# Where the code of three engines lies and in which order TensorE first enters it, in a decode block with a 512 MB cache

## The chip, the core and the metric

The kernel runs on one core of one Trainium2 chip, in one launch. The metric is the device time of one execution in microseconds; lower is better. Three executions of the kernel before took 1303.85 to 1303.99 us, with a median of 1303.93 us.

## The reference, cut to what matters

One decode step of a transformer block for B = 2 rows of D = 448, in float32: layer norm, attention with 16 heads of 256 over a cache of 8192 keys and values for each row, and then a second layer norm and a bilinear feed-forward layer of F = 1792.

```python
q = (layernorm(x) @ wq).reshape(B, 1, 16, 256).transpose(0, 2, 1, 3)
scores = einsum("bhqd,bhkd->bhqk", q, k_cache) * 256 ** -0.5
o = einsum("bhqk,bhkd->bhqd", softmax(scores), v_cache)
h = x + o.transpose(0, 2, 1, 3).reshape(B, 1, 4096) @ wo
n = layernorm(h)
out = h + ((n @ w_gate) * (n @ w_up)) @ w_down
```

There are 32 pairs of head and row. Each pair reads 8 MB of keys and 8 MB of values, and with the weights 561 MB have to come in.

## The kernel before, in words

All large loads are issued by SyncE on one queue, in the order in which they are needed: the first weights `w[0]`, the first quarter of the keys of pair 0 (`k0a`) and the rest of them (`k0`), the keys of pair 1, and then values and keys in turn (`loads`, L381 and L190). SyncE waits ahead of some of them until a buffer is free. A load lies over 128 partitions, and it is spread over the core's 16 DMA engines.

**Start.** ScalarE loads `x`. TensorE turns it with four small transposes (L241), VectorE and TensorE make its mean and its variance (L244 to L266), and TensorE makes the queries of the first four heads (`query`, L272 and L277), which ScalarE scales (L285). VectorE multiplies the first quarter of the keys by the first query (L358, into `vb`), and SyncE waits for that product, `product[0]`, before it issues the keys of pair 1.

**Loop.** PE, VectorE and ScalarE each run a loop over the heads. VectorE multiplies keys by the query and sums over 256 (L358, L363); TensorE and ScalarE make the softmax; TensorE multiplies by the values (`mix`, L336). The two engines hand work to each other by semaphores that are counted down again (`take`, L319).

**End.** The last two pairs are written out without a loop. Of the last pair's 64 key blocks, ScalarE sums the first `BY_ACT` = 44 by 44 single activations with an accumulated output (L529), VectorE the other 20 (L363). SyncE waits for both sums, `last_act[0]` and `summed_last`, because the last values and the weights of the feed-forward layer go into the buffer `kb`, in which the last keys lie. After that come the last values in three parts (`LAST`, on the semaphores `late`), `wg`, `wu` in two halves and `wd` in four parts (`DOWN` = 7, 4, 2, 1). TensorE's last work is the product with `wd` (L778); VectorE copies `y` (L785), and SyncE stores it (L796).

**Code and blocks.** An engine's program is loaded in blocks. The numbers that the code uses are 256 instruction slots for a block of TensorE and 128 for one of VectorE or ScalarE. In the kernel before, TensorE's loop begins at the head of its second block (`head_slot={PE: 0}`), all that stands ahead of it lies in its first block, and the end of the program follows behind the loop. VectorE's and ScalarE's code lies where it falls.

Of the kernel before, what the change touches and what calls it, by code (L numbers as in the profile page):

```python
# [4 lines left out]
AF = mybir.ActivationFunctionType  # L5
ALU = mybir.AluOpType
AX = mybir.AxisListType
PE, DVE, ACT = (getattr(mybir.EngineType, n) for n in ("PE", "DVE", "Activation"))

B, D, H, SK, DH, F = 2, 448, 16, 8192, 256, 1792  # L10
EPS = 1e-5
P = 128
HALF = 64
DC = 4
# [3 lines left out]
HC = 16  # L18
# [9 lines left out]
BY_ACT = 44  # L28
# [45 lines left out]
def decode_block(nc, x, k_cache, v_cache, w, wg, wu, wd, out):  # L74
# [4 lines left out]


    names = ("x", "w", "k0", "k1", "k0a", "v", "g", "p", "d", "a", "zero", "dp", "ap", "pd", "pa", "da")
    names += ("dd", "aa", "gp", "first", "mixed", "heads")
    S = {n: Sem(nc, n) for n in names}
    late = [Sem(nc, f"late{i}") for i in range(len(LAST) + 1 + 2 + len(DOWN))]
    done = Sem(nc, "out")
    pe, dve, act, sp, pool = (
        Engine(e) for e in (nc.tensor, nc.vector, nc.scalar, nc.sync, nc.gpsimd)
    )

    def p_(instr):  # L90
        return S["p"].by(instr)

    def v_(instr):
        return S["d"].by(instr)

    def a_(instr):
        return S["a"].by(instr)
# [4 lines left out]
    def place(name, shape, offset=None):  # L102
        size = 4
        for n in shape[1:]:
            size *= n
        if offset is None:
            offset = at[0]
            at[0] += -(-size // 32) * 32
        return nc.alloc_sbuf_tensor_at(name, list(shape), F32, offset=offset).ap()
# [9 lines left out]
    ident = place("ident", (P, P))  # L119
# [3 lines left out]
    s_t = [place(f"s{i}", (P, NJ)) for i in range(2)]  # L123
# [15 lines left out]
    x_sb = place("x_sb", (B, DC * P))  # L139
# [30 lines left out]
    xT_ps = banks[6][:, : DC * B].rearrange("p (c b) -> p c b", b=B)  # L170
# [9 lines left out]
    def k_at(i, lo=0, hi=NJ):  # L180
        first = i % 2 * (NJ - OVER)
        return kb[:, first + lo : first + hi, :]


    x_in = S["x"].by(nc.scalar.dma_start(x_sb[:, :D], x.rearrange("b s d -> (b s) d")), 16)
    w_in = {0: S["w"].by(nc.sync.dma_start(wb[:, WQ:], w[0][:, WQ:]), 16)}

    def load_k(i, lo=0, hi=NJ, sem=None):
# [6 lines left out]
    t = S["g"].by(nc.gpsimd.memset(ident, 0.0))  # L195
    pool.wait(t)
    g_id = S["g"].by(
        nc.gpsimd.affine_select(
            out=ident, in_=ident, compare_op=ALU.not_equal, fill=1.0, base=0,
            pattern=[[-1, P]], channel_multiplier=1,  # L200
        )
    )
# [33 lines left out]
    )  # L236
    dve.wait(x_in)
    t = v_(nc.vector.tensor_copy(x_sb[:, D:], x_sb[:, D - HALF : D]))
    pe.wait(g_id, x_in, t)
    for c in range(DC):  # L240
        got = nc.tensor.transpose(xT_ps[:, c, :], x_sb[:, c * P : (c + 1) * P], ident[:B, :B])  # L241
    t = p_(got)
    dve.wait(t)
    t = v_(nc.vector.tensor_copy(xT, xT_ps))  # L244
    dve.wait(t)
    t = over_chunks(sum_x, xT)
    pe.wait(v_ones, t)
    t = p_(nc.tensor.matmul(mean_ps, ones, sum_x, start=True, stop=True))
    dve.wait(t)
    t = v_(  # L250
        nc.vector.scalar_tensor_tensor(
            xc, mean_ps[:, None, :].to_broadcast([P, DC, B]), -1.0 / D, xT,
            op0=ALU.mult, op1=ALU.add,
        )
    )
    dve.wait(t, g_xb)
    x_spread = spread(xb, xc, P)
    t = v_(nc.vector.tensor_mul(sq, xc, xc))
    dve.wait(t)
    t = over_chunks(sum_sq, sq)  # L260
    pe.wait(t)
    t = p_(nc.tensor.matmul(var_ps, ones, sum_sq, start=True, stop=True))
    act.wait(t, v_eps)
    t = a_(nc.scalar.activation(std, var_ps, AF.Sqrt, bias=eps_t, scale=1.0 / D))
    dve.wait(t)
    t = v_(nc.vector.reciprocal(rstd, std))  # L266
# [47 lines left out]
    def behind(i, k):  # L314

        return S["p"], P0 + ORDER.index((i - (NQ - B), k)) + 1

    def take(e, sem, n=1):
        e.wait_ge(S[sem].h, n).then_inc(S[sem].h, -n)  # L319

    def tell_of(instr, sem):
        instr.then_inc(S[sem].h, 1)
# [10 lines left out]
    def mix(lo, hi, v, own=0):  # L333
        for t in range(lo // 2, hi // 2):
            g, j = 32 * (t % 4), 2 * t - lo
            got = nc.tensor.matmul(  # L336
                o_ps[own][g : g + 2, :], p_t[own][:, 2 * t : 2 * t + 2], v[:, j : j + 2, :],
                start=(t < 4), stop=(t >= NJ // 2 - 4),
            )
        return got  # L340
# [12 lines left out]
    last_act = []  # L353
    last = NQ - 1
    queries = qb.rearrange("p h b d -> p (h b d)")

    def keys_times(kt, q, to=None):
        return nc.vector.tensor_mul(  # L358
            kt if to is None else to, kt, q[:, None, :].to_broadcast([P, kt.shape[1], DH])
        )  # L360
# [55 lines left out]
    first = v_(summed(0, NJ - HC, NJ, vb[:, :HC, :]))  # L416
    take(nc.vector, "k0", 16)
    t = v_(keys_times(k_at(0, 0, NJ - HC), qb[:, 0, 0]))
    dve.wait(t)
    t = v_(summed(0, 0, NJ - HC, k_at(0, 0, NJ - HC)))  # L420
# [4 lines left out]
    with nc.Fori(0, H - 1, engines=[DVE]) as g:  # L425
        for n in (1, 2):
            b = n % B
            off = nc.vector.snap((g + n // 2) % HEADS * (B * DH))
            q = queries[:, bass.ds(off + b * DH, DH)]
            parts = ((0, HC), (HC, NJ)) if b else ((NJ - HC, NJ), (0, NJ - HC))  # L430
            kt = k_at(n, *parts[0])
# [8 lines left out]
            kt = k_at(n, *parts[1])  # L440
# [7 lines left out]
    t = v_(  # L448
        nc.vector.tensor_reduce(
            sel16, ident.rearrange("p (g b r) -> p b r g", b=B, r=R)[:, :, 0, :],  # L450
            axis=AX.X, op=ALU.add,
        )
    )
# [5 lines left out]
    t = v_(  # L459
        nc.vector.tensor_scalar(  # L460
            share, sel16[:, None, :].to_broadcast([P, DC + 1, B]), -1.0 / D, None, op0=ALU.mult
        )
    )
# [12 lines left out]
    q = qb[:, (H - 1) % HEADS, B - 1]  # L476
    take(nc.vector, "k1", 16)
    dve.wait(behind(last - 1, 0))
    told["nm", last - 1] = v_(negated())
    ready = [v_(keys_times(k_at(last, 0, HC), q))]  # L480
    dve.wait(behind(last - 1, 2))
    d_rl[last - 1] = v_(nc.vector.reciprocal(rl_t[0], l_ps))
    for lo in range(HC, NJ, HC):
        ready.append(v_(keys_times(k_at(last, lo, lo + HC), q)))
    dve.wait(ready[-1])
    summed_last = v_(summed(last, BY_ACT, NJ, k_at(last, BY_ACT, NJ)))


# [1 line left out]
    with nc.Fori(0, H - 1, engines=[ACT]) as g:  # L490
        for b in range(B):
# [9 lines left out]
            got = turned_out(b, 0)  # L501
        tell_of(got, "ap")
        off = nc.scalar.snap(g % HEADS * (B * DH))
        for b in range(B):
            take(nc.scalar, "pa")
            got = nc.scalar.activation(  # L506
                queries[:, bass.ds(off + b * DH, DH)], q_ps[b], AF.Copy, scale=rstd[:, b : b + 1]
            )
# [14 lines left out]
        told["oT", i] = a_(turned_out(k, k))  # L523

    ends(last - 1)
    for k in range(BY_ACT):
        act.wait(ready[k // HC])
        kt = k_at(last)[:, k, :]
        t = a_(nc.scalar.activation(kt, kt, AF.Copy, accum_out=s_t[1][:, k : k + 1]))  # L529
    last_act.append(t)  # L530
    summed_at[last] = summed_last
    dve.wait(last_act[0], summed_last)
    told["m", last] = v_(highest(last))
# [6 lines left out]
        nc.gpsimd.sem_inc(S["gp"].h, HEADS)  # L540


    with nc.Fori(0, H - 1, engines=[PE], head_slot={PE: 0}) as g:
        with nc.Fori(0, B, engines=[PE]):
            take(nc.tensor, "dp")
            tell_of(top(), "pd")
            take(nc.tensor, "dp")
            tell_of(bias(), "pa")
            take(nc.tensor, "ap")
            tell_of(whole(), "pd")  # L550
            take(nc.tensor, "v", 16)
            tell_of(mix(0, NJ, vb), "pa")
            take(nc.tensor, "ap")
            tell_of(turned(), "pa")
        take(nc.tensor, "ap")
        take(nc.tensor, "gp")
        off = nc.tensor.snap(g % HEADS * WH)
        for c in range(2):
            nc.tensor.matmul(  # L559
                acc_ps, oT.rearrange("p c b r -> p c (b r)")[:, c], wb[:, bass.ds(off + c * D, D)],  # L560
                start=False, stop=False,
            )
        for b in range(B):
            tell_of(query(off, b), "pa")
# [4 lines left out]
    v_parts, lo = [], 0  # L569
    for n in LAST:  # L570
# [3 lines left out]
        to = kb[:, lo : lo + n, :]  # L574
# [9 lines left out]
    wd_in, lo = {}, 0  # L584
# [44 lines left out]
    pe.wait(told["p", last])  # L629
    p_(whole())  # L630
    p_(mix(56, NJ, vb[:, 56:]))
    pe.wait(v_o)
    for k, (lo, hi, v, there) in enumerate(v_parts[:-1]):
        pe.wait(there)
# [11 lines left out]
    lo, hi, v, there = v_parts[-1]  # L646
# [24 lines left out]
    def group(w, q):  # L671
# [8 lines left out]
        start=True, stop=False,  # L680
    )
    dve.wait(t_hq)
    t = v_(nc.vector.tensor_mul(mean_h, share, total[:, None, :].to_broadcast([P, DC + 1, B])))  # L683
    pe.wait(t)
    t = p_(
        nc.tensor.matmul(
            xc_ps.rearrange("p c b -> p (c b)"), ones, mean_h.rearrange("p c b -> p (c b)"),
            start=False, stop=True,
        )
    )  # L690
# [9 lines left out]
    t = v_(nc.vector.tensor_copy(xc_h, xc_ps[:, :DC]))  # L700
    dve.wait(t)
    t = v_(nc.vector.tensor_mul(sq_h, xc_h, xc_h))
    dve.wait(t)
    t = over_chunks(sum_h, sq_h)
# [30 lines left out]
        )  # L735

    t_var = []
    pe.wait(t_xr, wg_in, v_blank)
    t_g = project(g_ps, wg_t, FG, variance)
    dve.wait(t_var[0])  # L740
    t = v_(nc.vector.tensor_scalar_add(ve, varh_ps, EPS))
# [30 lines left out]
    for k in range(NF):  # L772
        n, g = FF[k]
# [3 lines left out]
        for q in range(YN):  # L777
            got = nc.tensor.matmul(  # L778
                y_ps[32 * q : 32 * q + 32, :],
                hmT[n // 2][:, n % 2, g].rearrange("p b r -> p (b r)"),  # L780
                wd_t[:, k, q * YW : (q + 1) * YW], start=False, stop=(k == NF - 1),
            )
    t = p_(got)
    dve.wait(t)
    t = v_(nc.vector.tensor_copy(y, y_ps))  # L785
# [10 lines left out]
    t = done.by(nc.sync.dma_start(rows, eight(y)), 16)  # L796
# [60 lines left out]
```

## Time and profile before

| | |
|---|---|
| median of three runs | 1303.93 us (1303.85 to 1303.99) |
| the profiled execution | 1303.78 us |
| its span, from the first to the last instruction | 1302.5 us |
| VectorE busy | 1121.5 us, 86% of the span |
| TensorE busy (matmuls) | 494.4 us, 38% |
| ScalarE busy | 86.9 us, 7% |
| moved by DMA | 561.31 MB, 431 GB/s over the span |

The profiled execution took 1.28 us more than its span. Its time is 0.15 us below the median of the runs. Names such as `bank` stand for PSUM tiles, `kb` and `vb` for the buffers of keys and values, `wb` for attention weights. The suffix q (SPq, ACTq, PEldq) means the part of an engine that issues its instructions.

### The profile page before, as it was taken

The page shows a single profiled execution, that of the slowest core. Times are in us where ns is not written, and L with a number is a line of the kernel's source. Part 1 is how long each engine was busy: PE and PEld are TensorE (multiplying, and loading weights), DVE is VectorE, ACT ScalarE, POOL GpSimd, SP SyncE. Part 2 cuts the span into 40 slices and gives each one's busy share as a digit, 9 for nine tenths or more (in the row PEclk, how much of TensorE's full clock was granted, in tenths as well). Part 3 has the DMA queues.
Part 4 walks back from the last instruction along what each step waited for, and adds up shares of the span by engine and source line. Part 5 has one row for each costly group of instructions (what it writes and reads, how often), then busy time and mean ns, then how long its engine had stood idle before and what let it go on. Part 6 is the DMA issues. An engine that isn't in the chain of part 4 may idle for free. (4 is left out here: it accounts for less than half of the span.)

```text
span 1302.5 us, 7994 instructions
## 1 busy us (share of the span) xinstructions
PE 494.4 (38%) x3182; PEld 200.4 (15%) x3182; DVE 1121.5 (86%) x272; ACT 86.9 (7%) x293; POOL 1.3 (0%) x8
## 2 busy tenths in 40 slices
PE   5034314343331433415343043432334333253548
PEld 5011102111110111202121021210112001020213
DVE  5998888889988699888899868998888897888970
ACT  2000000000000000000000000000000000000060
POOL 0000000000000000000000000000000000000000
PEclk9566657676666765667676576765667666676668
DMA  9999999999999999999999999999999999999998
GB/s 409 447 425 433 427 443 421 449 421 449 421 449 435 419 441 429 429 441 421 449 421 449 435 421 449 419 443 427 433 437 423 431 451 427 431 439 423 447 416 368
DMA packets 11412, 561.31 MB, mean 431 GB/s; under 512 B 1290, under 2 KB 1420, under 8 KB 1676
## 3 DMA queue, kind: packets, MB, share of 16 engines
q1 hardware_dynamic: 11400, 561.20, 99.7%
q8 instruction: 5, 0.08, 0.0%
q14 instruction: 3, 0.02, 0.0%
q10 hardware_dynamic: 4, 0.00, 0.0%
HBM read 561.19 MB, written 0.01 MB: 431 GB/s over the span
## 5 line engine op out<-in xcount | busy, mean ns | idle before, releaser
L358 DVE TENSOR_TENSOR kb<-kb,qb 128x12288 f32<-128x12288 f32 (+1 forms) x65 | 551.4, 8486 | 125.8 <-DVEq L319 125.7
L363 DVE TENSOR_REDUCE s<-kb 128x48 f32<-128x12288 f32 (+2 forms) x62 | 539.6, 8704 | 4.4
L336 PE MATMUL bank<-vb,p 128*2 128x512 f32 x1984 | 284.2, 734 | 408.5 <-PEq L319 408.5
L336 PEld LDWEIGHTS bank<-vb,p 128*2 128x2 f32 x1984 | 53.2, 96 | 610.6 <-issue 610.5
L328 PE MATMUL bank<-nm,ones 1*128 1x1 f32 x64 | 17.1, 334 | 202.8 <-PEq L319 202.4
L498 ACT ACTIVATE o_sb<-bank 128x512 f32<-128x512 f32 x30 | 17.9, 597 | 693.8 <-ACTq L319 693.8
L272 PE MATMUL bank<-wb,xb 128*128 (+1 forms) x228 | 60.7, 405 | 0.8 <-DMA wb<-in_w_dram 0.8
L325 PE MATMUL bank<-ident,m 128*1 128x128 f32 x32 | 10.3, 322 | 111.3 <-PEq L319 111.3
L328 PEld LDWEIGHTS bank<-nm,ones 1*128 1x128 f32 x64 | 15.3, 294 | 212.2 <-issue 210.8
L272 PEld LDWEIGHTS bank<-wb,xb 128*128 128x128 f32 x228 | 42.6, 201 | 19.9 <-issue 14.4
L345 PE MATMUL bank<-sel,o_sb 128*128 128x1 f32 x256 | 32.8, 249 | 29.9 <-PEq L319 29.1
L345 PEld LDWEIGHTS bank<-sel,o_sb 128*128 128x128 f32 x256 | 31.0, 191 | 58.8 <-issue 57.1
L559 PE MATMUL bank<-wb,oT 128*32 x60 | 32.6, 677 | 14.4 <-PEq L319 14.4
L331 PE MATMUL bank<-lsum,ones 128*128 128x1 f32 x64 | 17.4, 342 | 30.6 <-PEq L319 29.9
L372 ACT ACTIVATE nb<-bank 128x1 f32<-128x1 f32 x32 | 5.5, 171 | 330.0 <-ACTq L319 325.1
L277 PEld LDWEIGHTS bank<-wb,xb 128*128 128x128 f32 x152 | 23.7, 197 | 2.2
L277 PE MATMUL bank<-wb,xb 128*128 (+1 forms) x152 | 23.7, 279 | 0.0
L331 PEld LDWEIGHTS bank<-lsum,ones 128*128 128x128 f32 x64 | 15.6, 302 | 33.3 <-issue 32.4
L506 ACT ACTIVATE qb<-bank,rstd 128x256 f32 x30 | 14.2, 474 | 92.6 <-ACTq L319 92.6
L325 PEld LDWEIGHTS bank<-ident,m 128*1 128x1 f32 x32 | 2.6, 82 | 114.5 <-issue 114.5
L529 ACT ACTIVATE kb<-kb 128x256 f32<-128x256 f32 x44 | 17.6, 405 | 3.4 <-DVE kb L358 3.4
L683 DVE TENSOR_TENSOR mean_h<-share,total 128x10 f32<-128x10 f32 x1 | 0.2, 170 | 14.8 <-ACT hq L675 14.8
(100 smaller groups left out, 135.1 us busy)
## 6 DMA issues: line engine op xcount, KB each, us to landing
wb<-in_w_dram SPq DMA_DIRECT2D x3, 3584.0 KB, 37.5
kb<-in_A_k_cache_dram SPq DMA_DIRECT2D x1, 6144.0 KB, 25.3
kb<-in_A_v_cache_dram SPq DMA_DIRECT2D x1, 4096.0 KB, 31.9
wb<-in_w_dram SPq DMA_DIRECT2D x2, 1792.0 KB, 20.1
kb<-in_B_w_gate_dram SPq DMA_DIRECT2D x1, 3136.0 KB, 20.8
kb<-in_A_v_cache_dram SPq DMA_DIRECT2D x1, 3072.0 KB, 11.8
kb<-in_A_k_cache_dram SPq DMA_DIRECT2D x1, 2048.0 KB, 11.2
vb<-in_B_w_up_dram SPq DMA_DIRECT2D x1, 1792.0 KB, 20.0
```

Source lines behind the costliest of these rows:

```text
L272: nc.tensor.matmul(q_ps[b], xb[:, c, b, :], wb[:, bass.ds(off + WQ + c * DH, DH)], start=(c == 0), stop=False,)
L277: got = nc.tensor.matmul(q_ps[b][:, k * P : (k + 1) * P], xb[:, DC - 1 + k, b, :], wb[:, bass.ds(off + WQ + (DC - 1) * DH, P)], start=Fals ...
L328: return nc.tensor.matmul(nb_ps, ones[:1, :], nm, start=True, stop=True)
L331: return nc.tensor.matmul(l_ps, ones, lsum, start=True, stop=True)
L336: got = nc.tensor.matmul(o_ps[own][g : g + 2, :], p_t[own][:, 2 * t : 2 * t + 2], v[:, j : j + 2, :], start=(t < 4), stop=(t >= NJ // 2 - 4),)
L345: got = nc.tensor.matmul(oT_ps[:, c : c + 1], o_sb[:, (2 * k + c) * P : (2 * k + c + 1) * P], sel[:, k : k + 1], start=(k == 0), stop=(k = ...
L358: return nc.vector.tensor_mul(kt if to is None else to, kt, q[:, None, :].to_broadcast([P, kt.shape[1], DH]))
L363: return nc.vector.tensor_reduce(s_t[i % 2][:, lo:hi], kt, axis=AX.X, op=ALU.add)
L498: tell_of(nc.scalar.activation(o_sb, o_ps[0], AF.Copy), "ap")
L506: got = nc.scalar.activation(queries[:, bass.ds(off + b * DH, DH)], q_ps[b], AF.Copy, scale=rstd[:, b : b + 1])
L529: t = a_(nc.scalar.activation(kt, kt, AF.Copy, accum_out=s_t[1][:, k : k + 1]))
L559: nc.tensor.matmul(acc_ps, oT.rearrange("p c b r -> p c (b r)")[:, c], wb[:, bass.ds(off + c * D, D)], start=False, stop=False,)
```

## The change

Four things are changed. VectorE's and ScalarE's code begins 128 slots behind a boundary of 256, that is in a second block of 128, by `addr_align` with an `offset` of 128; ScalarE's load of `x` stands ahead of that. TensorE begins with a branch into its third block, goes on from there to its fourth (`look`), and then to the head of its second block, where the four transposes of `x` now stand; from there it goes back to where it began, and runs the rest in order. `head_slot` of its loop goes from 0 to 20, behind that code. Where the program comes past the two landing places, it branches over them. VectorE now waits for the transposes on a semaphore `xt`. ScalarE's 44 activations become a loop of 11 turns with 4 activations each, which takes one count of `ka` a turn; VectorE raises `ka` by 4, 4 and 3 with its products. VectorE's and SyncE's waits for ScalarE's sums are on a semaphore `summed` with 11 counts.

```diff
     x_in = S["x"].by(nc.scalar.dma_start(x_sb[:, :D], x.rearrange("b s d -> (b s) d")), 16)
+    nc.vector.addr_align(256, offset=128, max_nops=0)
+    nc.scalar.addr_align(256, offset=128, max_nops=0)
+
+    def goto(label, here=None):
+        nc.br(label, engines=[PE])
+        if here is not None:
+            nc.switch_bb(here, parent=None)
+
+    def look(k, to):
+        goto(f"behind{k}", f"block{k}")
+        nc.tensor.wait_ge(S["g"].h, 1)
+        goto(to, f"behind{k}")
+
+    goto("block2", "start")
     w_in = {0: S["w"].by(nc.sync.dma_start(wb[:, WQ:], w[0][:, WQ:]), 16)}
...
-    pe.wait(g_id, x_in, t)
-    for c in range(DC):
-        got = nc.tensor.transpose(xT_ps[:, c, :], x_sb[:, c * P : (c + 1) * P], ident[:B, :B])
-    t = p_(got)
-    dve.wait(t)
+    x_there = (g_id, x_in, t)
+    dve.wait((S["xt"], 1))
...
-    ready = [v_(keys_times(k_at(last, 0, HC), q))]
+    keys_times(k_at(last, 0, HC), q).then_inc(S["ka"].h, HC // 4)
...
     for lo in range(HC, NJ, HC):
-        ready.append(v_(keys_times(k_at(last, lo, lo + HC), q)))
-    dve.wait(ready[-1])
+        got = keys_times(k_at(last, lo, lo + HC), q)
+        if lo < BY_ACT:
+            got.then_inc(S["ka"].h, min(HC, BY_ACT - lo) // 4)
+    dve.wait(v_(got))
...
-    for k in range(BY_ACT):
-        act.wait(ready[k // HC])
-        kt = k_at(last)[:, k, :]
-        t = a_(nc.scalar.activation(kt, kt, AF.Copy, accum_out=s_t[1][:, k : k + 1]))
-    last_act.append(t)
+    flat_k = k_at(last).rearrange("p j d -> p (j d)")
+    with nc.Fori(0, BY_ACT // 4, engines=[ACT]) as g:
+        take(nc.scalar, "ka")
+        to = nc.scalar.snap(g * 4)
+        off = nc.scalar.snap(g * (4 * DH))
+        for k in range(4):
+            kt = flat_k[:, bass.ds(off + k * DH, DH)]
+            got = nc.scalar.activation(kt, kt, AF.Copy, accum_out=s_t[1][:, bass.ds(to + k, 1)])
+        tell_of(got, "summed")
+    last_act.append((S["summed"], BY_ACT // 4))
...
-    with nc.Fori(0, H - 1, engines=[PE], head_slot={PE: 0}) as g:
+    nc.tensor.addr_align(256, max_nops=0)
+    goto("queries", "block1")
+    for sem, n in x_there:
+        nc.tensor.wait_ge(sem.h, n)
+    for c in range(DC):
+        got = nc.tensor.transpose(xT_ps[:, c, :], x_sb[:, c * P : (c + 1) * P], ident[:B, :B])
+    tell_of(got, "xt")
+    turn = nc.alloc_registers("turn", engines=[PE])
+    nc.regs_mov(turn, 0)
+    nc.br_lt(turn, 1, on_true="start", on_false="queries", engines=[PE])
+    nc.switch_bb("queries", parent=None)
+    with nc.Fori(0, H - 1, engines=[PE], head_slot={PE: 20}) as g:
...
     p_(mix(56, NJ, vb[:, 56:]))
+    look(2, "block3")
     pe.wait(v_o)
...
     t_var = []
+    look(3, "block1")
     pe.wait(t_xr, wg_in, v_blank)
```

The rows below are the instructions of an engine in the order in which they stand in its program, with the line that makes them, what they write and read, and how often they repeat. First, TensorE ahead of its loop in the kernel before: the transposes of `x` are its first work, and behind the last matmul (`x_acc`, L302) come an alignment and the entry of the loop.

```order
L241 MATMUL bank<-ident,x_sb 128x2 x4
L248 MATMUL bank<-sum_x,ones 128x2
L262 MATMUL bank<-sum_sq,ones 128x2
L272 MATMUL bank<-wb,xb 128x256 x3
...
L302 MATMUL bank<-x_sb,rows 32x448
L543 ISA
L543 UNCONDITIONAL_BRANCH
L544 UNCONDITIONAL_BRANCH
```

The same place in the changed kernel.

```order
L194 UNCONDITIONAL_BRANCH
L264 MATMUL bank<-sum_x,ones 128x2
...
L318 MATMUL bank<-x_sb,rows 32x448
L566 ISA
L194 UNCONDITIONAL_BRANCH
L571 MATMUL bank<-ident,x_sb 128x2 x4
L575 COMPARE_AND_BRANCH
L577 ISA
L577 UNCONDITIONAL_BRANCH
L578 UNCONDITIONAL_BRANCH
```

The transposes now stand behind `x_acc`, at the head of the second block, and are reached by branches. Next, TensorE behind the loop in the changed kernel, at the two places where it branches over a landing place (each L194 row holds that branch and the landing place's own).

```order
L352 MATMUL bank<-vb,p_59 2x512 x4
L194 UNCONDITIONAL_BRANCH x2
L352 MATMUL bank<-kb,p_60 2x512 x16
...
L721 MATMUL bank<-mean_h,ones 128x10
L694 MATMUL bank<-wb,oT 32x112 x4
L194 UNCONDITIONAL_BRANCH x2
L754 MATMUL bank<-kb,xb 32x512 x2
```

The matmuls around them are those of before, in the same order. Last, ScalarE between the softmax of the pair before the last and that of the last pair, before:

```order
L372 ACTIVATE nb<-bank 128x1
L375 ACTIVATE p_59,lsum<-s_57,nb 128x64
L529 ACTIVATE kb,s_58<-kb 128x256 x44
L372 ACTIVATE nb<-bank 128x1
L375 ACTIVATE p_60,lsum<-s_58,nb 128x64
```

And now, where an ISA row sets an address from a register:

```order
L545 UNCONDITIONAL_BRANCH
L551 ISA
L551 REGISTER_ALU
L551 ACTIVATE kb,s_58<-kb 128x256
L551 ISA
L551 ACTIVATE kb,s_58<-kb 128x256
...
L545 REGISTER_ALU
L545 COMPARE_AND_BRANCH
```

The 44 activations have become a body of 4 (two of the four are left out here), with four such address rows, a register sum, the loop's own sum and its branch.

## Rows read from the trace of the kernel before

**Rows 1.** Page: span, share of the 16 DMA engines in 40 slices, bytes.
```profile
span 1302.5 us, 7994 instructions
DMA  9999999999999999999999999999999999999998
HBM read 561.19 MB, written 0.01 MB: 431 GB/s over the span
```

**Rows 2.** Chain that ended last: start us, us, what; its last pieces.
```profile
1271.19 28.21 DMA vb<-in_wd_dram
...
1299.44 0.99 PE bank L778 x24
...
1300.46 0.28 DVE y L785
```

**Rows 3.** Page, DMA queues: packets, MB, share of 16 engines.
```profile
q8 instruction: 5, 0.08, 0.0%
q14 instruction: 3, 0.02, 0.0%
```

**Rows 4.** Queues in 28.8-28.9, 1261.6-1261.7, 1294.0-1294.1, 1299.7-1299.9, 1273.4-1273.6 us (packets begun there).
```profile
q8 instruction: 1, 0.02, 64.2%
q8 instruction: 1, 0.02, 63.5%
q8 instruction: 1, 0.02, 67.1%
q8 instruction: 1, 0.02, 31.6%
q14 instruction: 1, 0.01, 10.0%
```

**Rows 5.** DMA view of 1296 to 1302 us, GB/s in 40 slices of 0.15 us.
```profile
GB/s 311 454 311 430 502 358 526 311 442 311 359 382 353 257 215 173 167 120 119 111 99 72 48 0 0 109 0 0 0 0 0 0 0 0 0 0 0 0 0 3
```

**Rows 6.** Line L543, TensorE's loop, its branch: ns min/median/max, first and last start.
```profile
L543 PEldq COMPARE_BRANCH  x16: 83/218/315, 25.1 to 1235.6; - x16
```

**Rows 7.** Windows, 1257.9 us to the end: busy us (x instructions) of each engine.
```profile
1257.90:1302.50 44.60, 39.00 (x415) 15.63 (x415) 11.09 (x26) 7.75 (x32) 0.00 (x0) 0.84 0.91 384
```

**Rows 8.** Timeline of the first 30 us: start, us, instruction [idle before <-releaser].
```profile
0.74 0.39 SPq L186 DMA_DIRECT2D wb<-in_w_dram  x1
1.19 16.02 SPq L190 DMA_DIRECT2D kb<-in_A_k_cache_dram  x3
2.45 0.55 PE L241 MATMUL bank<-ident,x_sb 2*128 2x2 f32 x4 [2.45 <-DVE x_sb L238]
7.58 2.93 PE L272 MATMUL bank<-wb,xb 128*128 128x256 f32 x6 [0.79 <-DMA wb<-in_w_dram]
12.43 4.43 DVE L358 TENSOR_TENSOR vb<-kb,qb 128x4096 f32<-128x4096 f32 x1 [5.15 <-DMA kb<-in_A_k_cache_dram]
27.08 12.96 DVE L358 TENSOR_TENSOR kb<-kb,qb 128x12288 f32<-128x12288 f32 x1 [5.22 <-DVEq L319]
```

**Rows 9.** DMA view of 0 to 2 us, 40 slices of 0.05 us.
```profile
DMA  0000000000000000000000000000000002099999
```

**Rows 10.** Lines L529, L490, L506 on ScalarE: ns min/median/max, first and last start.
```profile
L529 ACT ACTIVATE kb<-kb x44: 400/404/417, 1244.6 to 1261.8; 128x256 f32<-128x256 f32 x44
L490 ACTq COMPARE_BRANCH  x15: 40/45/50, 132.1 to 1239.0; - x15
L506 ACTq FUSED_REGOPS  x30: 52/69/96, 130.2 to 1238.8; - x30
```

**Rows 11.** Timeline of 1222 to 1265 us: VectorE's last sums, SyncE's loads around them.
```profile
1235.66 28.30 SPq L381 DMA_DIRECT2D kb<-in_A_v_cache_dram  x3
...
1257.64 5.49 DVE L363 TENSOR_REDUCE s<-kb 128x20 f32<-128x5120 f32 x1
...
1264.01 0.43 SPq L581 DMA_DIRECT2D kb<-in_B_w_gate_dram  x1
```

**Rows 12.** Page, DMA issues: KB, us from issue to landing.
```profile
kb<-in_A_v_cache_dram SPq DMA_DIRECT2D x1, 4096.0 KB, 31.9
```

More of the change, by code (lines that the diff above doesn't have):

```diff
@@ L81, in decode_block @@
     names = ("x", "w", "k0", "k1", "k0a", "v", "g", "p", "d", "a", "zero", "dp", "ap", "pd", "pa", "da")
-    names += ("dd", "aa", "gp", "first", "mixed", "heads")
+    names += ("dd", "aa", "gp", "first", "mixed", "heads", "ka", "summed", "xt")
     S = {n: Sem(nc, n) for n in names}
```

## Prediction

> **What bounds the kernel now.** I read the page first, then the chain of waits, then the DMA queues. The page's strip has every slice but the last at 9 tenths or more of 16 DMA engines, at 431 GB/s over 1302.5 us [rows 1]. The chain that ended last goes back through the landing of `wd`, waited for over 28.21 us up to 1299.40; behind it stand only 0.99 us of TensorE and 0.28 us of VectorE and the store [rows 2]. So the time is set by when the stream of loads begins, by gaps in it, and by when its last engine is done. One of 16 engines moves 431 / 16 = 26.9 GB/s.
>
> The change touches code loading, and that is in the trace: a queue of kind "instruction" with five packets of 0.08 MB together (16 KB each), and another with three of 8 KB [rows 3]. The narrow windows place them: 16 KB at 28.8, 1261.6, 1294.0 and 1299.7 us (the fifth, at 1278.8, reads the same), 8 KB at 1273.4 (two more at 1241 and 1243). A share of 64.2% of 16 engines for 0.1 us is 1.03 us of one engine; 10.0% for 0.2 us is 0.32 us [rows 4]. In those times that engine brings no data.
>
> The end of the stream shows it. From 1298.25 us the rate is 173 GB/s, 6.4 engines; at 1298.55 to 1299.0 it is 120 to 111, some four; then 99, 72, 48, and nothing from 1299.45 [rows 5]. Four engines are late by about 1 us, and four 16 KB packets came before that; about three more are late by less, and three were of 8 KB. That is an inference from the counts. Bytes after 1297.95 us: the ten slices sum to 1381 GB/s, times 0.15 us is 207 KB, which 16 engines move in 0.48 us. Level engines would be done at 1298.43, 1.0 us earlier, and without the eight packets' own time (5.1 us of one engine before the end, a sixteenth of it is 0.3) at 1298.1. **So everything that code loading costs in this stream is 1.0 to 1.3 us, 0.1% of the time.**
>
> The Trainium skill, "Runtime: NRT & Kernel Launch", section "Instruction fetch mechanics", calls the cost of crossing a block boundary mostly hidden. By that sentence the sum would be 0. The rows agree for the engine that executes, and differ for the DMA engines by the 1 us above.
>
> **The change part by part.**
>
> *TensorE's early visits.* Its loop is entered at 25.1 us [rows 6] and a packet follows at 28.8, so I read a packet as the load of the next block when a block is entered. From 1257.9 to the end there are 415 matmul and 415 weight-load records [rows 7], 830 slots, a bit over three blocks of 256: that fits the entries behind 1261.6, 1278.8, 1294.0 and 1299.7. The change enters the third and the fourth block early, so it should move the packets of 28.8, 1261.6 and 1278.8 (blocks three to five) to the start. Nothing enters the fifth block early. The packet for the sixth, near 1294, stays, and one engine stays 1.03 us or more late to the end. The last, at 1299.7, falls behind the stream and costs nothing in either kernel.
>
> Moving a packet gains only if it leaves the stream. Data flows from 1.7 us on [rows 9]; TensorE is released at about 0.7. The issue of `w` at 0.74 had its first data 1.0 us later, so the first early packet may begin just ahead of the stream, and the others fall into it. An engine delayed at 3 us is as late at the end as one delayed at 28.8, for no slice between shows the queue empty [rows 1]. Gain: between 0 and 0.3 us (the latest engine at 1299.45 against the first of the four at about 1299.15), since one late engine suffices; I take 0.1 to 0.2.
>
> *What the visits cost at the start.* The price of a branch to a block that is not there is in no row. Bounds: from 0 to the loaded case, 28.8 - 25.1 + 1.03 = 4.8 us for each. The first has an empty queue, nearer to 1.0 + 1.0 = 2 us; the fourth block may be on its way by then. I take 4 us in all for TensorE. It then turns `x` at 6.5 instead of 2.45 us; 0.79 us of this vanish in its wait for `w` [rows 8], and the queries are some 3.2 us late. Behind them: `product[0]` at 12.43, SyncE's keys of pair 1 (the third issue ends at 1.19 + 16.02 = 17.21, so it begins at 16.9), then the values. VectorE waits for the rest of the first keys until 27.08 [rows 8], so the queue holds data until about 26.3; less 1.0 us from issue to data, the issue could come at 25.3. The cover is about 8.4 us. A delay of 3.2 costs nothing. Without that cover it would cost its full length.
>
> *VectorE and ScalarE in their second block of 128.* A branch at the start, and 8 KB packets that move from 1241 to 1273 us to the start. At 0.32 us they don't make the latest engine. 0, at most 0.3 either way.
>
> *ScalarE's loop.* Before, 44 activations ran from 1244.6 to 1261.8 us, 0.40 us apart, so four take 1.6 us. A turn adds four address settings of 69 ns and a branch of 45 [rows 10], with the count and two sums about 0.45 us of issuing. If that runs while the datapath works, 0; if none of it does, 11 x 0.45 = 5 us. The issue work is under a third of the 1.6 us, so I take 0 to 1 us. Cover: VectorE's sum ends at 1257.64 + 5.49 = 1263.13, some 0.9 us behind ScalarE, and SyncE waits for both. Of SyncE's three issues of values the last ends at 1263.96 [rows 11]; the two behind the wait begin near 1263.2. The part ahead of them landed at 1235.66 + 31.9 = 1267.6 [rows 11, 12]; its leading engines run dry about 1.8 us earlier (they lead by 1.4, and the landing is told a little late), so data must be issued by 1264.8, 1.6 us of cover. The late engines have 1.4 us more, and they set the end. ScalarE may lose 0.9 + 1.6 + 1.4 = 3.9 us before the end moves.
>
> *The two branches over the landing places* cost 83 to 315 ns on TensorE [rows 6]; from 1271 us on the chain waits for DMA [rows 2]. 0.
>
> Sum, for the profiled execution's 1303.78 us (span 1302.5 and 1.28 around it): -0.15 +- 0.3, 1303.6. The runs' median lies 0.15 above that execution: **1303.7 us**.
>
> **The rivals.**
>
> *A, the stream becomes level.* The early packets fall ahead of 1.7 us or into a part where engines have time to spare, and the one near 1294 goes too, because blocks once asked for ahead are kept in another way than I think. All 1.0 to 1.3 us come back: 1302.7 us. For it: the window before 1.7 us is empty [rows 9]. Against it: it is only 1 us long, as long as one packet, and the sixth block.
>
> *B, slower: TensorE keeps only two blocks.* Then the way back to the second block and from there to the first are misses under load. TensorE loses 2 + 1 + 4.8 + 4.8 = 12.6 us, `product[0]` about 11.5, and the keys of pair 1 come 11.5 - 8.4 = 3 us after the queue is empty: 1306.9 us. It decides from 8.4 us of delay on; below that it is invisible. The late packets would all be there again. No row shows how many blocks TensorE keeps: in the trace it never goes back further than its loop's head. The same section of the Trainium skill says that a taken branch to a target outside the current two-page window forces a fetch before execution goes on; by that sentence B is what happens. The section also gives TensorE 128 KiB, room for eight blocks, by which B doesn't. No run here shows either yet.
>
> *C, slower: ScalarE's issue work isn't hidden.* 5 us less 3.9 is 1.1 us: 1304.9. The rows' longest values (96 and 50 ns) make 5.8 us and 1305.7. It passes 0.2% only from 6.5 us on.
>
> *The change doesn't do what it says:* the late packets come in spite of the early visits. The time is then that of before, inside the forecast's own range.
>
> **How the numbers follow.** The forecast (no change, 1303.2 to 1304.2) gets 0.62, A 0.18, B 0.09, C 0.08, and 0.03 for what I haven't seen. The predicted time is the forecast's. The range goes from A's end, 1302.5, to between C's two prices, 1305.3: it holds the forecast, A and most of C, and leaves out B's upper part. 0.2% is 2.6 us, about what a measurement of this kernel can tell from no change. No case reaches 2.6 us of gain, so faster gets 0.03 of doubt alone; slower gets 0.06 of B, 0.03 of C and 0.02 of the unseen, 0.11; same the rest, 0.86.
>
> **What would show it.** Right: 16 KB packets in the first 10 us, none between 28 and 1290, one near 1294; the transposes at 4 to 8 us; `product[0]` later but no slice under 9 tenths near 26 us; the rate after 1298.5 us still that of one to four engines until 1299.2 or later; ScalarE's 44 activations done by 1263. Wrong: the keys of pair 1 issued after 25.3 us and a slice under 9 tenths behind it (B), the second part of the last values issued after 1266 us (C), or the stream ending at full rate at 1298.3 (A).

## The result and the profile after

The changed kernel takes **1306.39 us** (median of 21 runs, 1304.76 to 1308.41), the kernel before 1304.01 us in the same runs (1303.76 to 1305.09). The ratio is 1.0019, 95% interval 1.0013 to 1.0024: 2.4 us slower, above the range of the prediction. The runs also spread over 3.7 us.

The page of the profiled execution (1307.19 us) answers to [rows 1]; the chain that ended last answers to [rows 2] (start us, us, what).

```profile
span 1305.9 us, 8107 instructions
DMA  9999999999999999999999999999999999999998
HBM read 561.19 MB, written 0.01 MB: 430 GB/s over the span
```

```profile
1273.19 29.60 DMA vb<-in_wd_dram
...
1302.83 1.00 PE bank L814 x24
...
1303.86 0.28 DVE y L821
```

The page's strip shows nothing. The stream still sets the end, and `wd` lands at 1302.79 us instead of 1299.40. So I looked for the first place where this stream is late. TensorE's branches come first, by the time in which each began (0 to 2, 4 to 5, 9 to 10.3 us, then the branch back to the start): ns min/median/max, first and last start.

```profile
L194 PEldq COMPARE_BRANCH  x1: 3842/3842/3842, 0.8 to 0.8; - x1
L194 PEldq COMPARE_BRANCH  x1: 5552/5552/5552, 4.7 to 4.7; - x1
L194 PEldq COMPARE_BRANCH  x1: 181/181/181, 10.3 to 10.3; - x1
L575 PEldq COMPARE_BRANCH  x1: 244/244/244, 10.9 to 10.9; - x1
```

The third block holds TensorE for 3.84 us and the fourth for 5.55; the two ways back cost 0.18 and 0.24. The queues of code in narrow windows answer to [rows 4]: packets begun at 1.8, 7.9, 13.7, 1294.7 and 1303.3 us (16 KB), and at 3.4 and 5.6 us (8 KB).

```profile
q8 instruction: 1, 0.02, 97.1%
q8 instruction: 1, 0.02, 55.2%
q8 instruction: 1, 0.02, 56.1%
q8 instruction: 1, 0.02, 67.1%
q8 instruction: 1, 0.02, 58.0%
q14 instruction: 1, 0.01, 12.2%
q14 instruction: 1, 0.01, 9.7%
```

Code thus moved as planned, and the packet near 1294 stayed. The timeline of the start answers to [rows 8] (start, us, instruction [idle before <-releaser]):

```profile
10.67 0.56 PE L571 MATMUL bank<-ident,x_sb 2*128 2x2 f32 x4 [10.67 <-issue]
14.93 2.91 PE L288 MATMUL bank<-wb,xb 128*128 128x256 f32 x6
19.23 4.42 DVE L374 TENSOR_TENSOR vb<-kb,qb 128x4096 f32<-128x4096 f32 x1 [3.66 <-ACT qb L301]
28.58 12.94 DVE L374 TENSOR_TENSOR kb<-kb,qb 128x12288 f32<-128x12288 f32 x1
64.01 0.33 SPq L209 DMA_DIRECT2D kb<-in_A_k_cache_dram  x1
135.72 4.42 DVE L374 TENSOR_TENSOR kb<-kb,qb 128x4096 f32<-128x4096 f32 x1 [9.88 <-DVEq L335]
```

The same two last rows in the kernel before:

```profile
62.53 0.33 SPq L190 DMA_DIRECT2D kb<-in_A_k_cache_dram  x1
133.86 4.42 DVE L358 TENSOR_TENSOR kb<-kb,qb 128x4096 f32<-128x4096 f32 x1 [9.49 <-DVEq L319]
```

VectorE's multiplication of the first keys came at 28.58 us for 27.08 [rows 8], with none of the 5.22 us of idle time ahead of it. It does not stop there: VectorE goes from one piece to the next without a pause until its first sum of pair 1, which frees the buffer, and on which SyncE waits to issue the **keys of pair 2**: 64.01 us for 62.53. The keys of pair 3, on whose landing VectorE waits, start it at 135.72 for 133.86. So 1.9 of the 3.4 us that separate the two profiled executions exist by 134 us.

Between the two lies an empty queue. A packet's row does not name its engine, but on one engine a packet begins when the one ahead of it ends, so begins and ends can be paired. By them, four engines that have brought their values of pair 0 by 66.6 us stand idle until 67.0 to 67.3, and eleven wait up to 0.4 us near 26 us, where the keys of pair 1 were issued at 23.7. Before, no engine waited over 0.01 us at either place.

The packets behind the gap are slow as well. The packets begun from 66 to 70 us (count, MB, share of 16 engines), first in the changed kernel, where 5 of the 25 are under 512 B, then in the kernel before, where 1 of the 29 is:

```profile
q1 hardware_dynamic: 25, 1.31, 90.6%
q1 hardware_dynamic: 29, 1.84, 105.9%
```

The other 20 are of 64 KB and took 2.90 us each; the 28 of before took 2.42.

The other 1.5 us of the 3.4 arise at the end. The rate from 1297 to 1303 us in 40 slices of 0.15 us answers to [rows 5]:

```profile
GB/s 382 466 335 382 442 358 382 442 406 311 478 358 430 370 388 353 221 245 155 167 119 143 143 60 131 72 119 36 36 24 24 48 24 24 24 12 24 36 24 0
```

From 1301.3 us on one engine is at work alone. Its packets, followed back, lead to the 16 KB of code at 1294.7 us, and that engine was late already: near 1259 us four engines end their 64 KB packets over 1.1 us behind the other twelve, and near 1293 us four are late again, this one among them.

### The profile page after: what moved, and what is told of

It reads as the page before. It is cut to its first block, busy times and chain, and to the rows that moved or that the text cites. A ratio compares the mean times of both kernels' runs of the same rounds, so it can differ in the third digit from the quotient of the medians.

```text
span 1305.9 us, 8107 instructions
## 1 busy us (share of the span) xinstructions
PE 499.0 (38%) x3182; PEld 201.4 (15%) x3182; DVE 1121.1 (86%) x272; ACT 86.9 (7%) x293; POOL 1.3 (0%) x8
## 5 line engine op out<-in xcount | busy, mean ns | idle before, releaser
L341 PE MATMUL bank<-ident,m 128*1 128x128 f32 x32 | 10.3, 322 | 108.1 <-PEq L335 108.1
L361 PE MATMUL bank<-sel,o_sb 128*128 128x1 f32 x256 | 32.8, 249 | 29.9 <-PEq L335 29.1
L593 PE MATMUL bank<-wb,oT 128*32 x60 | 35.6, 732 | 14.4 <-PEq L335 14.4
L347 PE MATMUL bank<-lsum,ones 128*128 128x1 f32 x64 | 17.4, 342 | 30.6 <-PEq L335 29.9
L551 ACT ACTIVATE kb<-kb x44 | 17.6, 401 | 3.6 <-ACTq L335 3.6
L385 DVE TENSOR_REDUCE nm<-bank 1x1 f32<-1x128 f32 x32 | 8.7, 272 | 4.9 <-PE bank L341 4.9
```

Source lines behind the costliest of these rows:

```text
L347: return nc.tensor.matmul(l_ps, ones, lsum, start=True, stop=True)
L361: got = nc.tensor.matmul(oT_ps[:, c : c + 1], o_sb[:, (2 * k + c) * P : (2 * k + c + 1) * P], sel[:, k : k + 1], start=(k == 0), stop=(k = ...
L551: got = nc.scalar.activation(kt, kt, AF.Copy, accum_out=s_t[1][:, bass.ds(to + k, 1)])
L593: nc.tensor.matmul(acc_ps, oT.rearrange("p c b r -> p c (b r)")[:, c], wb[:, bass.ds(off + c * D, D)], start=False, stop=False,)
```

## The experiments

Theory 1: the late issue of the keys of pair 2 (and a little of pair 1) empties the queue. Theory 2: the early packets alone make engines late, to the end. Theory 3: VectorE's and ScalarE's new code costs by itself. All runs, and from the profiled execution (us): VectorE's start on the first keys, the issue of pair 2's keys, the idle time of the 16 engines together between the last packets of pair 0's values and the next load (about 65 us; before under 0.1, after 5.4), and VectorE's start on pair 3:

| | median (range) | ratio (95%) | first keys | issue | idle | pair 3 |
|---|---|---|---|---|---|---|
| visits alone | 1305.96 (1305.24-1306.94) | 1.0015 (1.0006-1.0024) | 28.61 | 64.06 | 9.5 | 135.41 |
| rest alone | 1305.41 (1304.09-1306.94) | 1.0009 (1.0000-1.0018) | 27.62 | 63.06 | 3.9 | 134.34 |
| one visit | 1305.49 (1304.74-1306.24) | 1.0012 (1.0003-1.0021) | 28.38 | 63.82 | 8.8 | 134.75 |
| late by keys | 1307.85 (1306.85-1308.71) | 1.0028 (1.0018-1.0038) | 30.34 | 65.77 | 16.4 | 138.06 |
| late by weights | 1304.15 (1303.86-1304.75) | 1.0001 (0.9992-1.0010) | 26.99 | 62.44 | under 0.1 | 133.95 |
| idle visits | 1303.91 (1303.77-1304.54) | 1.0000 (0.9991-1.0009) | 27.25 | 62.70 | under 0.1 | 133.90 |
| three idle visits | 1303.96 (1303.68-1304.07) | 0.9998 (0.9989-1.0008) | 27.09 | 62.53 | under 0.1 | 133.91 |
| before, w first | 1303.89 (1303.74-1304.09) | 0.9999 (0.9990-1.0008) | 27.47 | 62.92 | none | 133.82 |
| after, w first | 1304.47 (1304.23-1306.25) | 1.0004 (0.9995-1.0013) | 29.29 | 64.71 | none | 134.25 |
| rest, w first | 1303.94 (1303.81-1304.21) | 0.9999 (0.9990-1.0008) | 27.54 | 62.99 | none | 133.96 |
| after, both | 1303.92 (1303.81-1304.20) | 0.9998 (0.9988-1.0007) | 28.67 | 64.11 | none | 133.71 |

The kernel before had medians of 1303.91 to 1303.95 us beside them. The interval of rest alone reaches down to no change; its loss is read together with its run with w first, below.

**Visits alone.** The kernel before with `goto("block2", "start")`, the moved transposes and the two `look` calls of the change.

> The kernel before with TensorE's early visits alone (branches into the third and fourth block, transposes of x in the second); VectorE's and ScalarE's code and ScalarE's 44 activations stay as before. Theory 1 (the two visits to absent blocks hold TensorE for 3.84 and 5.55 us, all that hangs on the queries comes late, and the load queue runs empty near 26 and 65 us): all of the loss is here, 1306.0 to 1306.8 us. Theory 2 (code packets that fall on an engine already late make the end later, whatever the start does): also 1306 or more. Theory 3 (ScalarE's loop or the place of VectorE's and ScalarE's code): 1304.0.

1305.96: 2.0 of the 2.4 us, at the low edge of what was expected. No engine waited near 26 us here, where the keys of pair 1 were issued at 23.2, so the gap near 65 us is enough.

**Rest alone.** The change without those lines.

> The changed kernel without TensorE's visits: its transposes and its loop head as before, but VectorE's and ScalarE's code in the second block of 128 and ScalarE's loop of 11 turns. Theories 1 and 2: 1303.7 to 1304.2 us, and ScalarE's activations still 0.40 us apart. Theory 3: 1306 us.

Missed: 1305.41. VectorE's rows show why, with the issue behind them:

```profile
2.74 0.18 DVE L256 COPY x_sb<-x_sb 2x64 f32<-2x64 f32 x1 [0.69 <-DMA x_sb<-in_A_x_dram]
27.62 12.96 DVE L376 TENSOR_TENSOR kb<-kb,qb 128x12288 f32<-128x12288 f32 x1 [5.21 <-DVEq L337]
63.06 0.33 SPq L208 DMA_DIRECT2D kb<-in_A_k_cache_dram  x1
```

The 5.21 us of idle time ahead of the first keys are whole, so VectorE did not come late: the keys did, by 0.54 us. Their load has landed when its latest engine is done, and by its packets that is the engine on which 8 KB of code fell at 3.54 us (the 8 KB of 5.59 us lie on another). They took 0.31 us, and the packet of data behind them 1.07 us where others of its size took 0.54, so that engine lost 0.84 us. An engine can also be late without any code: in "before, w first" the first keys came 0.39 us later than in the kernel before. With the issue at 63.06 two engines have no data until 66.3 and 67.1 us, and the spread between engines behind pair 2's keys is 2.17 us (1.79 before). The rest of this execution's loss came at the end: the 16 KB packet of TensorE's fourth block, at 1262.8 us, met an engine already 2.1 us late, and TensorE began on the second part of the last values at 1277.04 us instead of 1274.96.

```profile
1277.04 6.51 PE L354 MATMUL bank<-kb,p 128*2 128x512 f32 x32 [2.09 <-DMA kb<-in_A_v_cache_dram]
```

So theory 2 has a part, behind theory 1's.

**One visit.** The changed kernel, with the fourth block's visit taken out:

```diff
-    look(2, "block3")
+    look(2, "block1")
...
-    look(3, "block1")
```

> The changed kernel with one visit instead of two: TensorE enters the third block and goes from there to the second. Theory 1: one hold of about 3.8 us, transposes at about 5 us, product[0] no more than 3 us late, which is less than VectorE's 5.2 us of waiting before the rest of the first keys; no empty queue, 1303.7 to 1304.5 us. Theory 2: two packets (third and fourth block) still lie in the first 10 us and two more near 1279 and 1294, so 1305 to 1306.5 us.

1305.49, a time that theory 2 had named, and the first keys are waited for until 28.38, 1.3 us longer than before:

```profile
13.73 4.43 DVE L374 TENSOR_TENSOR vb<-kb,qb 128x4096 f32<-128x4096 f32 x1 [3.98 <-DMA kb<-in_A_k_cache_dram]
28.38 12.96 DVE L374 TENSOR_TENSOR kb<-kb,qb 128x12288 f32<-128x12288 f32 x1 [5.21 <-DVEq L335]
```

TensorE's lateness was within the cover here, and the early packets delayed the landing: the engine that brings the last of these keys carried 8 KB of code at 3.40 us and 16 KB at 7.52. Both theories had sent the loss down the wrong way: an early packet does not cost by being carried to the end, but by delaying the load that is waited for just then.

**Late by keys, late by weights.** No code moves. The transposes of the kernel before wait for a landing as well.

```diff
-    pe.wait(g_id, x_in, t)
+    pe.wait(g_id, x_in, t, k0a)        # late by keys
+    pe.wait(g_id, x_in, t, w_in[0])    # late by weights
```

> The kernel before, in which TensorE's transposes of x wait in addition for the landing of the first quarter of the keys (about 12.4 us instead of 2.45); no code moves, no packet of code moves. Theory 1: product[0] about 8.8 us late, so the keys of pair 1 come about 2 us after the queue is empty, and the keys of pair 2 another 1.6 us late: 1306.5 to 1307.6 us. Theory 2: 1304.0 us, since no code packet has moved.

> The kernel before, but the transposes wait for the first weights (7.4 us) too: the early chain is later by some 3.5 us and no code moves. Theory 1: VectorE idles 5.2 us ahead of the first keys, so 3.5 us are covered: the keys of pair 2 are issued at 62.5 us, 1303.8 to 1304.3. If the chain's lateness cost in proportion (5.2 us late cost 3.9 us in the run where the transposes waited for the first part of the keys): about 1306.

Late by keys made the kernel 3.9 us slower with its code where it was: the issue alone does it. Not all of it arose at 26 and 65 us: the queue runs empty once more near 1269 us (20 us of the engines together; visits alone 6.2, the changed kernel 1.1, before 0.1), behind SyncE's wait for the sums of the last keys. Late by weights, with the product for `product[0]` begun at 16.17 for 12.43, cost nothing that can be measured; 1.39 of the 5.22 us were left:

```profile
26.99 12.96 DVE L358 TENSOR_TENSOR kb<-kb,qb 128x12288 f32<-128x12288 f32 x1 [1.39 <-DVEq L319]
62.44 0.33 SPq L190 DMA_DIRECT2D kb<-in_A_k_cache_dram  x1
```

**Idle visits, three idle visits.** The transposes stay. The visits stand between TensorE's queries and its loop:

```diff
+    pe.wait(t_k0)                  # idle visits: VectorE has multiplied the first keys
+    goto("block2", "queries")      # third and fourth block; the other kernel: no wait, fifth too
```

> The kernel before with TensorE's visits to its third and fourth blocks, made only when VectorE has multiplied the first keys (about 40 us), where TensorE has nothing to do until 53 us; the transposes stay where they were. Same code packets as the visits-only kernel, two of them 35 us later. Theory 1: the start is undisturbed, the keys of pair 2 are issued at 62.5 us, no gap near 65 us, 1303.8 to 1304.4. Theory 2 (packets on engines make them late wherever they fall): 1305.3 to 1306.5.

> The kernel before with three visits of TensorE (third, fourth and fifth block) between its queries and its loop, 25 to 45 us, where it has nothing to do, so that fewer code packets fall among the last transfers. If the packet near 1294 us sets the end: 1303.0 to 1303.6. If it falls on an engine with time to spare: 1303.8 to 1304.2. If the packets at 30 to 45 us make engines late to the end: above 1304.8.

Neither costs anything. Idle visits has its packets at 45.7, 52.9 and 60.1 us, and its branches held TensorE for up to 7.87 us. Packets behind the first keys are free in these two; that refutes theory 2 in its plain form. Three idle visits has 16 KB packets at 28.8, 36.0, 43.1, 50.5 and 1299.6 us and none between the last two, and ends at the time of before: moving the packet near 1294 within the stream gains nothing.

**w first, and both.** SyncE issues the second weight load (8.8 us of stream) ahead of the keys of pair 2.

```diff
             load_v(0)
+            load_w(1)
...
-            if off == 0 and k < H // HEADS:
-                sp.wait((S["heads"], k * HEADS) if k else q_first)
+            if off == 0 and 0 < k < H // HEADS:
+                sp.wait((S["heads"], k * HEADS))
```

> The kernel before with the same exchange of two loads. In the kernel before the queue does not run empty near 65 us, though it comes close; both theories: 1303.5 to 1304.3. Above 1305 would say that the exchange itself costs, and would take its meaning from the other run.

> The changed kernel as it is, but SP issues the second weight load (3.67 MB, 8.8 us of the stream) ahead of the keys of pair 2 instead of behind them. Theory 1 (the loss is a queue that runs empty near 65 us, because the keys of pair 2 wait for VectorE's first sum of pair 1, which comes 1.5 us late): the 8.8 us in the queue cover the lateness, no gap near 65 us, 1303.8 to 1304.6. Theory 2 (the early code packets alone make engines late to the end): 1305.5 to 1307, as the changed kernel.

> The kernel with the change's rest and no visits of TensorE (it lost 1.1 us, which I had not expected), with the exchanged weight load. Theory 1: its loss too is the late issue of pair 2's keys (63.06 us for 62.53), behind first keys that landed late on the engine that the two 8 KB packets at 3.8 and 5.8 us held up: 1303.7 to 1304.2. Theory 3 (VectorE's and ScalarE's new code costs by itself): 1304.9 to 1305.6, as without the exchange.

The exchange costs the kernel before nothing, takes the rest's loss away whole, and leaves 0.6 us of the change's. The profiled execution of the latter (1306.25 us) was the slowest of its 11, so its rows show more than its median lost; engines wait up to 0.7 us near 26 us, and nowhere from 62 to 78. For that one, the last kernel also issues a quarter of the first values ahead of the keys of pair 1 (`VA` = 48):

```diff
         if n == 0:
+            load_v(0, VA, NJ, vb[:, VA:], next(sems))
             sp.wait(product[0])
...
-            load_v(0)
+            load_v(0, 0, VA, vb[:, :VA])
+            load_w(1)
```

> The changed kernel with the exchanged weight load, and with the last quarter of the first values (2.1 MB, 4.9 us of the stream, into rows that nothing uses yet) issued ahead of the keys of pair 1, so that the queue has work at 26 us as well when those keys are issued late. Theory 1 (every loss is a queue that runs empty): neither gap is left, 1303.7 to 1304.2. If the 0.5 us that the exchange alone left over come from early packets rather than from the gap near 26 us: 1304.4 again.

1303.92, as before. SyncE's issues in it, and VectorE's start on pair 3:

```profile
3.61 0.55 SPq L398 DMA_DIRECT2D vb<-in_A_v_cache_dram  x1
23.78 0.33 SPq L210 DMA_DIRECT2D kb<-in_A_k_cache_dram  x1
64.11 0.33 SPq L210 DMA_DIRECT2D kb<-in_A_k_cache_dram  x1
133.71 4.42 DVE L375 TENSOR_TENSOR kb<-kb,qb 128x4096 f32<-128x4096 f32 x1 [3.31 <-DVEq L336]
```

Both keys are issued as late as in the changed kernel, and all of its code moves are in it; the stream is no longer late. Without the two empty stretches nothing of the loss is left. (The kernel before with both exchanges was not run; w first alone gains it nothing.) No version beat the kernel before by more than can be measured.

## Why the prediction was wrong

**The step that failed is "What the visits cost at the start"**, in the first three points below, and beside it the 0 for VectorE's and ScalarE's code.

- *The price.* I took 4 us for two visits; TensorE lost 9.5 us, and `x` was turned at 10.67 us instead of my 6.5. The bound of 4.8 for each was itself short: one visit took 5.55. My 6.5 also adds the 4 us to 2.45, though the visits run while TensorE would have waited for `x`: begun at 0.8 us, 4 us of them end at 4.8 (one visit, held for 3.64 us, turned `x` at 4.86).
- *The cover.* I counted 8.4 us up to the issue of pair 1's keys and stopped there. The next load in SyncE's order waits for VectorE, whose idle time ahead of the first keys (5.22 us, a row that I had shown) is the only slack on that way, and behind it there is almost none: an issue at 62.70 us cost nothing, one at 63.06 did. `product[0]` came 6.8 us late, 1.6 us more than that idle time, and pair 2's keys 1.5 us late.
- *Issue to data.* I took 1.0 us, from the first load into an empty queue. Pair 2's keys, issued at 64.01 while the values of pair 0 were still coming, reached their last four engines at 67.0 to 67.3: over 3 us. At pair 1's keys, too, 23.2 us was early enough (visits alone) and 23.7 was not, so the cover there was 6.4 to 6.8 us and not 8.4.
- *The code of VectorE and ScalarE.* I took 0, at most 0.3, from 0.32 us for a packet of 8 KB. The time behind a packet was missing: the packet of data behind it takes longer, mostly by 0.5 us, so that the engine that set the first keys lost 0.84 us in rest alone, which was 1.5 us slower in all. In the kernel before, the 64 KB behind the code of 28.8 us, begun between 29.8 and 29.9 us, took 2.90 us (181.2% of 16 engines for 0.1 us) where others took 2.42, so that a packet of 16 KB cost its engine 1.5 us and not 1.03:

```profile
q1 hardware_dynamic: 1, 0.07, 181.2%
```

The sentence "an engine delayed at 3 us is as late at the end as one delayed at 28.8" holds for the end only. In the first 27 us there is a load that VectorE waits for, and its landing is that of the latest engine.

**Rival B** gave nearly the measured time, 1306.9, for a wrong reason. The ways back to the second block and to the first, for which the trace has no packet, took 0.18 and 0.24 us against 3.84 and 5.55 for the third and fourth, so at least four blocks were kept. The Trainium skill, "Runtime: NRT & Kernel Launch", section "Instruction fetch mechanics", lets a taken branch to a target outside a two-page window force a fetch; this trace disagrees for TensorE, and agrees with the 128 KiB that the same section gives it. The "decides from 8.4 us of delay on" of rival B should have been 5.2.

**Right:** the packets of blocks three to five moved, the one near 1294 stayed, and the last one fell behind the stream. ScalarE's loop is free, and **rival C** fell: its 44 activations run 0.40 us apart as in [rows 10], 2.3 us later with the stream.

```profile
L551 ACT ACTIVATE kb<-kb x44: 398/401/417, 1246.9 to 1264.1; - x44
```

**Rival A** did not come: the late engines are still there at the end. That the four late engines of [rows 5] come from four 16 KB packets was an inference from counts. The ends of pair 2's keys, near 85 us, bear it out: behind one 16 KB packet (before) one engine is 1.3 us behind the next, behind three (idle visits) three engines are over 1.1 us behind the others, behind four (three idle visits) four. No run had fewer than four such packets within the stream, so the price of 1.0 us for them at the end stays unproven. Why the runs of the changed kernel spread over 3.7 us was not settled either; that a late packet meets a late engine in some executions would do it, and was seen in two profiled executions, rest alone's and the changed kernel's.

## What to carry to other kernels

Where a stream of loads sets the time, follow a delay at the start past the first wait that hides it, to every later issue that depends on it, and compare each with the moment when the queue would run dry. A load lands with its latest engine, so what takes time from one DMA engine costs when that engine becomes the latest of a load that somebody waits for; here 16 KB of code at 1.8 and 7.5 us did (one visit), and at 36 to 60 us did not. Slack at such an issue can be bought by putting a load that waits for nothing ahead of it; here that took the whole loss away.

## What the hardware showed that I had not expected

- A branch to a code block that is not there held TensorE for 3.84 us with a nearly empty queue and for 5.55 to 7.87 us beside the stream, though its packet takes 0.9 to 1.6 us (changed kernel).
- The packet of data behind a packet of code took longer than others of its size, mostly by 0.5 us: 2.90 for 2.42 us at 29.8 us in the kernel before, 0.96 for 0.47 at 1295.8 in the changed one.
- A queue empty on three engines, for 0.2, 1.4 and 2.2 us, cost more than the gaps: the issue of pair 2's keys 0.53 us late (rest alone) cost 1.5 us in the median. The engines start again unevenly, and they stayed uneven for 1200 us (spread 2.17 us behind pair 2's keys, 2.10 us ahead of the last values). Where nearly all of them ran dry together (late by keys), the spread behind pair 2's keys was 1.0 us.
- The first packets behind such a gap are slow: 2.90 us for 64 KB where 2.42 is usual. Over the changed kernel's profiled execution the packets of data hold each engine 1.0 us longer on average than before, while the three gaps (26, 65 and 1267 us) are 0.6 us for each engine.
- From issue to data is not one number. In late by keys, with nearly all engines idle, the load issued at 65.77 us had 15 engines at work 0.95 to 1.75 us later. In the changed kernel four engines waited 3.0 to 3.3 us from the issue, and in rest alone one waited 4.1, beside engines that went on without a pause.
